# Loading q and k as bf16 through GpSimd's queue in place of fp32 loads and on-chip casts

## The chip, the cores and the metric

One Trainium2 chip, and of it one core with its engines TensorE (PE), VectorE (DVE), ScalarE (ACT), GpSimd (POOL) and SyncE (SP), and 16 DMA engines that all queues share. The metric is the device time of one execution in microseconds (us), lower is better. A ratio is the mean time of one kernel's fast runs over that of the other's fast runs of the same rounds, so it is not quite the ratio of the medians that stand beside it.

## The reference

Attention with a feature map, whose output is normalised, sent through two large matrices, and added back:

```python
def phi(x):                                  # per head, x is 576 x 64
    proj = einsum('bhsd,df->bhsf', x, w_phi)             # 64 -> 128
    proj = proj - max(abs(proj), axis=-1, keepdims=True)
    return concatenate([exp(proj), exp(-proj)], axis=-1)
q_p, k_p = phi(q), phi(k)                    # q, k, v: 8 x 8 x 576 x 64, fp32
kv, z = einsum('bhsf,bhsd->bhfd', k_p, v), sum(k_p, axis=2)
x = einsum('bhsf,bhfd->bhsd', q_p, kv) / (einsum('bhsf,bhf->bhs', q_p, z) + 1e-6)
x = x.transpose(0, 2, 1, 3).reshape(8, 576, 512)
xn = (x - mean) / sqrt(var + 1e-6) * g_ln
out = x + maximum(xn @ w_ch1, 0) @ w_ch2     # 512 -> 2048 -> 512
```

## The kernel before

The batch is taken in four pairs; a pair has eight units (a head of both batches, or two heads of one), so there are 32 units. A unit's rows are 8 main tiles (512 rows of each half) and a rest, the "tails". A planner in the kernel's own Python lays all instructions out: each operation states the engines that may do it, its estimated cost, what it reads and writes, and a rank; a table `OFF` moves single ranks. Each engine then runs its list strictly in order.

```python
def load_main(key, n, nu, rank, queue): ...   # fp32, SyncE's queue, for n >= 8 two units a load
def a_trans(u): ...        # units 0..7: TensorE turns the high halves of the fp32 tile

def a_trans_dma(u):        # units 8..31
    b16 = b16_bufs[n % 2]                       # two bf16 buffers
    def cast_main(engine, i):                   # i: q or k, 128 x 512
        cast(engine, b16[:, i * 512 : (i + 1) * 512]..., qk_bufs[u["g"] % NBUF][:, i : i + 1, u["hh"], :])
    def turn():
        nc.sync.dma_start_transpose(out=u["qkT"]..., in_=b16)
    add(("DVE", "ACT", "POOL"), (0.21, 0.19, 0.36), rank, cast_mixed, ...)        # tails
    for i in range(2):
        add(("DVE", "ACT", "POOL"), (0.61, 0.5, 0.98), rank, ... cast_main(engine, i), ...)
    dma("SP", rank, 1152, turn, ...)
...
def load_w2(n, V, gate): ...       # fp32 to bf16 during the load, GpSimd's queue, 512 KB
...
if n == EARLY:
    for j in range(NW):
        load_w2(j, -5 + j, [("came", "q", 5)])
    gate("w2", GATE)               # SyncE's loads for units 8.. wait until w2's first part is there
...
for key in "kqv":
    load_main(key, m, HG, rank, "SP")           # m = n + 4
```

On GpSimd's list stand also `vv`, the scaling of v (for both halves of each unit), and the puts of attention's result into `x`. Parts of one tile of x have to change partitions, by small copies `x<-xs` (32 KB each) on ACT's queue.

## Time and profile before

| | before |
|---|---|
| median of the first runs | 373.9 us |
| TensorE busy | 356.9 us, 96% |
| DVE, ACT, POOL busy | 292.2, 239.0, 175.5 us |
| main casts for units 8 to 31 | 48: 12 on DVE, 16 on ACT, 20 on POOL |
| POOL's issues | 8 weight loads, 780 ns each for those of w2 |
| TensorE's shown waits after the start | 5.9 us |

The page is read from the top: busy shares say who might be the bound, slices say when, and the views of waits and of the chain say what a wait of the bound engine ends on. In this kernel the two stretches before and after 140 us differ. Columns below: stretch, its length, busy us and count of PE, weight loads, DVE, ACT, POOL, then granted clock, share of the DMA engines, GB/s.

```profile
40.00:140.00 100.00, 95.55 (x1000) 63.40 (x1010) 88.09 (x204) 82.62 (x191) 69.55 (x146) 1.00 0.97 227
140.00:200.00 60.00, 57.24 (x611) 35.65 (x615) 53.67 (x115) 52.46 (x125) 40.74 (x80) 1.00 0.73 168
```

Up to 140 us the DMA column stands at 0.97; from there to 200 us at 0.73. It adds up the times of all packets as the profile records them. Packets can overlap, so it can pass 1 (it is 1.21 from 50 to 60 us); "full" below means a column near 1 or above. (Some matmuls are missing from this trace, so PE's 95.55 and 57.24 are a few us low.)

### The profile page before, as it was taken

The numbers are of one execution on the slowest core, as the hardware profiler recorded it, in microseconds if no ns is written. First come the engines' busy times: TensorE is split into PE (matmuls) and PEld (weight loads), VectorE is DVE, ScalarE is ACT, GpSimd is POOL, SyncE is SP. The second block draws the span as 40 slices with busy tenths as digits, with TensorE's granted clock in tenths as the row PEclk, the third lists the DMA queues.
The fourth block names the chain that finished last, engine by engine and source line by source line (L and its number), as shares of the span: only waits on it lengthen the run. The fifth ranks groups of instructions, "written<-read, shape, count | busy, mean of one in ns | idle before, by whom it ended". The sixth has DMA issues, their size and how long they took to land.

```text
span 373.1 us, 9310 instructions
## 1 busy us (share of the span) xinstructions
PE 356.9 (96%) x3510; PEld 229.7 (62%) x3548; DVE 292.2 (78%) x645; ACT 239.0 (64%) x569; POOL 175.5 (47%) x356
## 2 busy tenths in 40 slices
PE   8899998999999999989999999999999999999995
PEld 7789776666556556546656646666566555555543
DVE  6799988979599889989988898858687956454522
ACT  4798977568889999989878789835675540000000
POOL 2634848646668868746586754161728100000000
PEclk9999999999999999999999999999999999999999
DMA  6999399895999997596943439500100180110102
GB/s 184 274 200 338 63 205 286 248 265 123 257 260 221 249 256 207 158 208 153 223 80 90 130 98 176 120 8 24 56 2 31 36 204 0 42 45 30 56 28 87
DMA packets 92974, 53.38 MB, mean 143 GB/s; under 512 B 59392, under 2 KB 88448, under 8 KB 92928
## 3 DMA queue, kind: packets, MB, share of 16 engines
q1 hardware_dynamic: 87040, 48.19, 51.6%
q0 software_dynamic: 4224, 4.19, 6.8%
q10 hardware_dynamic: 1664, 0.39, 0.5%
q8 instruction: 28, 0.46, 0.5%
q14 instruction: 18, 0.15, 0.1%
HBM read 36.77 MB, written 9.44 MB: 124 GB/s over the span
## 4 chain that ended last, share of the span: by engine, by line
PE 70%; DMA 14%; DVE 6%; ACT 4%; SPq 2%; issue 2%; POOL 1%; DVEq 0%; ACTq 0%; POOLq 0%
PE hT_ps L1275 28%; PE ch_ps L1305 26%; DMA qkT<-b 4%; DMA qk<-in_k_dram 4%; PE n_bank L998 3%; PE num L1041 2%; PE pk L796 2%; PE pq L941 2%; SPq L509 2%; DMA xT<-xc 2%; DMA w<-in_moe_w_ch_dram 2%; DVE numc L1055 1%; DMA x<-xs 1%; DVE numc L1060 1%; PE pt L946 1%
## 5 line engine op out<-in xcount | busy, mean ns | idle before, releaser
L1275 PE MATMUL hT_ps<-xT,w 128*128 128x384 bf16 (+1 forms) x832 | 150.7, 313 | 2.9 <-ACT hT L1285 1.2
L1305 PE MATMUL ch_ps<-w,hT 128*128 128x512 bf16 (+1 forms) x554 | 138.8, 373 | 2.0 <-issue 0.3
L1275 PEld LDWEIGHTS <-w 128*128 128x128 bf16 x832 | 76.8, 98 | 49.7 <-issue 6.4
L1283 DVE TENSOR_SCALAR hT<-hT_ps 128x384 bf16<-128x384 f32 (+1 forms) x134 | 70.5, 529 | 42.5 <-PE hT_ps L1275 40.7
L1305 PEld LDWEIGHTS <-hT 128*128 128x128 bf16 x592 | 54.4, 98 | 45.7 <-issue 1.7
L1070 POOL TENSOR_TENSOR x<-numc,rden 128x192 bf16<-128x192 f32 (+4 forms) x112 | 49.5, 459 | 65.4 <-DVE rden L1064 60.3
L824 POOL TENSOR_TENSOR vv<-v,em 128x512 bf16<-128x512 f32 x59 | 61.6, 1047 | 31.0 <-ACT em L809 15.6
L812 ACT ACTIVATE eb<-pk 128x1024 bf16<-128x1024 f32 x64 | 64.8, 1041 | 7.2 <-DVE m L802 7.2
L1285 ACT ACTIVATE hT<-hT_ps 128x384 bf16<-128x384 f32 (+1 forms) x74 | 34.2, 467 | 53.6 <-PE hT_ps L1275 52.7
L965 ACT ACTIVATE ea<-pt 128x1024 bf16<-128x1024 f32 x56 | 57.3, 1035 | 12.2 <-PE pt L946 11.4
L802 DVE TENSOR_REDUCE m<-pk 128x8 f32<-128x1024 f32 x32 | 38.7, 1211 | 0.9 <-PE pk L796 0.9
L958 DVE TENSOR_REDUCE m<-pq 128x8 f32<-128x1024 f32 x28 | 34.1, 1217 | 2.9 <-PE pq L941 2.6
L1312 DVE SCALAR_TENSOR_TENSOR o<-ch_ps,rstd,x 128x512 f32<-128x512 f32 (+1 forms) x37 | 27.0, 731 | 10.2 <-PE ch_ps L1305 8.3
L1041 PEld LDWEIGHTS <-ea 128*128 128x128 bf16 x512 | 25.3, 97 | 7.3 <-issue 0.8
L1188 DVE BATCH_NORM_STATS2 st<-x 128x6 f32<-128x256 bf16 (+1 forms) x52 | 25.0, 512 | 2.4 <-DMA x<-xs 1.8
L998 PE MATMUL n_bank<-vv,eb 128*128 128x65 bf16 x512 | 26.8, 194 | 0.0
L712 POOL TENSOR_TENSOR b<-qk,one 128x512 bf16<-128x512 f32 x20 | 20.6, 1039 | 9.8 <-DMA qkT<-b 9.1
L837 POOL TENSOR_TENSOR vv<-vx,em 128x130 bf16<-128x130 f32 x60 | 24.2, 403 | 0.3 <-DMA vx<-in_v_dram 0.3
L998 PEld LDWEIGHTS <-eb 128*128 128x128 bf16 x512 | 22.3, 98 | 2.7
L1503 PE MATMUL n_bank<-wz 128*128 128x120 bf16 x295 | 22.8, 225 | 0.5 <-ACT KV L1007 0.5
L1212 ACT ACTIVATE xc<-x,mv 128x512 bf16<-128x512 bf16 x30 | 20.2, 719 | 2.4 <-DVE mv L1203 1.7
L1503 PEld LDWEIGHTS <-wz 128*128 128x128 bf16 x295 | 19.0, 103 | 1.1 <-issue 0.8
(92 smaller groups left out, 454.6 us busy)
## 6 DMA issues: line engine op xcount, KB each, us to landing
out_dram<-o SPq DMA_DIRECT2D x31, 256.0 KB, 2.8
qk<-in_k_dram SPq DMA_DIRECT2D x24, 256.0 KB, 4.4
v<-in_v_dram SPq DMA_DIRECT2D x24, 256.0 KB, 3.9
qk<-in_q_dram SPq DMA_DIRECT2D x24, 256.0 KB, 5.0
w<-in_moe_w_ch_dram POOLq DMA_DIRECT2D x8, 512.0 KB, 10.7
qk<-in_k_dram SPq DMA_DIRECT2D x4, 512.0 KB, 5.6
qk<-in_q_dram SPq DMA_DIRECT2D x4, 512.0 KB, 6.7
v<-in_v_dram SPq DMA_DIRECT2D x4, 512.0 KB, 5.0
```

Of the source, the lines that this page charges most:

```text
L802: nc.vector.reduce_max(out=u["m"][:, 1, 0:MX], in_=u["pk"], axis=AX.X, apply_absolute_value=True)
L812: nc.scalar.activation(u["EB"][:, t, 0:MX, :], u["pk"], AF.Exp, scale=(1.0, -1.0)[t])
L824: eng.tensor_tensor(out=u["vv"][:, t, 0:MX, 0:D], in0=vb[:, hh, :].rearrange("p (c d) -> p c d", d=D), in1=bcast(e[:, 0:MX], 2, D), op=ALU ...
L958: nc.vector.reduce_max(out=out, in_=ps, axis=AX.X, apply_absolute_value=True)
L965: nc.scalar.activation(u["EA"][:, t, :], u["pt", None], AF.Exp, scale=(1.0, -1.0)[t])
L998: nc.tensor.matmul(ps[:, t, c // 4, :], EB[:, t, c, :], vv[:, t, c, :], start=False, stop=(t == 0 and c == MX - 1), skip_group_check=True,)
L1070: nc.gpsimd.tensor_tensor(out=dst, in0=st["numc"][ps_, at, 0:D], in1=bcast(st["rden"][ps_, at], 2, D), op=ALU.mult,)
L1275: nc.tensor.matmul(st["ps"], w1_sb[:, kc, jj * P : (jj + 1) * P], xT_bufs[xj][:, kc : nt * KC : KC, :], start=(kc == 0), stop=(kc == KC - 1),)
L1283: nc.vector.tensor_relu(h_sb[:, 0 : nt * P], st["ps"])
L1285: nc.scalar.activation(h_sb[:, 0 : nt * P], st["ps"], AF.Relu)
L1305: nc.tensor.matmul(ch[t, c][:, cols], hT[jj][:, rt * P : (rt + 1) * P], w2_sb[:, jj, cols], start=(jj == 0), stop=(jj == JC - 1),)
L1503: nc.tensor.matmul(warm, wz, wz[:, 0:WN], start=False, stop=False, skip_group_check=True)
```

## The change

The intent: let the DMA engines convert q and k while they load, so that DVE, ACT and GpSimd are rid of 48 casts, and let nine bf16 places (three in each of the three fp32 tiles that the first pair no longer needs) replace two, so that a unit's data can be asked for long before its turn. The memory of the two bf16 buffers becomes a fourth v buffer. The core of the diff (line cuts by "..."; the whole table `OFF` is new as well, some 400 numbers, and lets the planner order the new work; two of the planner's rules for GpSimd's transfers changed with it):

```diff
-    NBUF = 3
+    NBUF, VB = 3, 4
...
-    b16_bufs = [consts.tile([P, ST], BF16, name=f"b16_{i}") for i in range(2)]
...
+    def place(n):
+        i = (n - QK_DMA) % (3 * NBUF)                      # QK_DMA is 8
+        return i, (i // 3 + 1) % NBUF
+    def b16_of(n): ...                                     # that place in qk_bufs, as bf16
+    def load_cast(key, n):
+        src = bass.AP(tensor=t.tensor, ..., ap=[[4 * D, P], [...], [1, 4 * D]])     # 256 rows of 1 KB
+        first = n < QK_DMA + 5
+        dma("POOL", -3.5 + 0.1 * (n - QK_DMA) if first else rk("load." + key, n), 256,
+            lambda: nc.gpsimd.dma_start(out=dst, in_=src),
+            r=[("came", "q", 5) if first else ("turned", n - 5)] + freed(n), w=[("b16", i, slot)],
+            us=0.6, ns=0.05)
...
-        for i in range(2):
-            add(("DVE", "ACT", "POOL"), (0.61, 0.5, 0.98), rank, lambda engine, i=i: cast_main(engine, i), ...)
...
-                load_w2(j, -5 + j, [("came", "q", 5)])
+                load_w2(j, (-5.0, -4.0, -3.25, -3.15)[j], [("came", "q", 5)])
...
-            for key in "kqv":
-                load_main(key, m, HG, rank, "SP")
+            load_main("v", m, HG, rank, "SP")
+        if H <= m < NU:
+            for key in "kq":
+                load_cast(key, m)
```

`us=0.6, ns=0.05`: the planner takes an issue to cost GpSimd 0.6 us and a packet 50 ns.

## The prediction

> **What bounds the kernel now.** I read the page's busy times and slices first, then the engines over three stretches, then the costliest groups, the waits, and the chain of waits.
>
> The page (busy time, share, count; then the span in 40 slices, in tenths):
>
> ```profile
> PE 356.9 (96%) x3510; PEld 229.7 (62%) x3548; DVE 292.2 (78%) x645; ACT 239.0 (64%) x569; POOL 175.5 (47%) x356
> ...
> PE   8899998999999999989999999999999999999995
> ...
> DMA  6999399895999997596943439500100180110102
> ```
>
> Busy time by stretch (PE, weight loads, DVE, ACT, POOL, clock, DMA share, GB/s):
>
> ```profile
> 40.00:240.00 200.00, 192.48 (x2002) 123.41 (x2022) 178.20 (x395) 170.04 (x392) 131.62 (x262) 1.00 0.81 188
> 240.00:300.00 60.00, 59.52 (x546) 35.32 (x553) 47.10 (x101) 35.35 (x85) 25.97 (x49) 1.00 0.12 35
> ```
>
> TensorE is the bound from 40 us to the end, at full clock; from 40 to 240 us the engines that feed it are not far behind (DVE 89%, ACT 85%, POOL 66%). The first 36 us are set by loads and the chain of the first heads: 295 warm-up matmuls (L1503, 22.8 us) fill them. The reader should then ask how much TensorE really lacks. The waits in which TensorE stood still:
>
> ```profile
> PE n_bank L993 <- DVE numc L1060: 1.9, 2, 1.7
> PE qkT_ps L645 <- DMA qk<-in_k_dram: 1.5, 2, 1.3
> PE hT_ps L1275 <- ACT hT L1285: 1.2, 1, 1.2
> ...
> PE hT_ps L1275 <- DVE hT L1283: 0.9, 1, 0.9
> PE n_bank L1041 <- ACT ex L771: 0.7, 1, 0.7
> ```
>
> After the start, shown waits come to only 5.9 us (1.9 + 1.2 + 0.9 + 0.7 + 0.4 + 0.3 + 0.3 + 0.2). The timeline of TensorE gives a second bound. Its first expert matmul starts at 36.7 us, its last ends at 365.2: 328.5 us. Back to back in the trace, four hT matmuls of 384 columns take 0.65 us, sixteen of 256 take 1.75, three of 512 take 0.65. So the expert part needs 640 x 0.1625 + 192 x 0.109 + 576 x 0.216 = 249 us, and attention of 28 head pairs about 2.43 us each (timeline near 140 us: q 0.55, kv 0.64, k 0.44, mixed 0.17, num 0.63) = 68 us. 328.5 - 317 leaves **11.5 us: the most that any relief of the other engines can give**, and part of it is small gaps at changes of matmul kind that no relief takes away.
>
> What the change touches:
>
> ```profile
> L712 POOL TENSOR_TENSOR b<-qk,one 128x512 bf16<-128x512 f32 x20 | 20.6, 1039 | 9.8 <-DMA qkT<-b 9.1 <-DMA qk<-in_k_dram 0.7
> L710 ACT CAST b<-qk 128x512 bf16<-128x512 f32 x16 | 10.0, 631 | 5.4 <-DMA qkT<-b 5.3
> L706 DVE TENSOR_REDUCE b<-qk 128x512 bf16<-128x512 f32 x12 | 8.1, 674 | 3.5 <-DMA qkT<-b 2.4 <-DMA qk<-in_k_dram 1.1
> L612 POOL DMA_DIRECT2D w<-in_moe_w_ch_dram x4 | 3.0, 780 | 0.0
> ```
>
> 48 main casts, with idle time before them that ends with a transpose: two bf16 buffers make each cast wait for the transpose of two head pairs earlier. The chain of waits passes there too:
>
> ```profile
> 41.72 5.92 DMA w<-in_moe_w_ch_dram
> 47.65 0.68 SPq L521
> 48.39 9.43 DMA qk<-in_k_dram
> ...
> 86.90 4.05 DMA qkT<-b
> ...
> 96.27 5.58 DMA qkT<-b
> ```
>
> The second pair's q and k start only when the first part of w2 has landed (SyncE's gate at 47.65).
>
> **What the Trainium skill says.** "DMA: Bandwidth & Descriptors", section "SWDGE vs HWDGE vs iDMA": a cast during a transfer goes only through GpSimd's queue, where software writes the descriptors. The trace agrees as far as it goes: the only casting loads, the weights, are issued by POOL and take 780 ns of it for 512 descriptors. The same page, "Issuing engines are not separate DMA queues": all queues share the same 16 DMA engines, so moving loads from SyncE saves issue time, not bandwidth. "SBUF — State Buffer", section "Who interferes with whom": a DVE instruction in a two-port mode (copy, cast, tensor_scalar from SBUF) shuts GpSimd out, descriptors included; tensor_reduce does not. Here only the few xc<-x instructions of the first pair (L1207, 340 ns) look like that, so I expect little of it. "Perfetto Trace Analysis", section "Identifying the Most-Contended Engine": matmul busy time is a poor measure of headroom. The trace agrees: 96% busy hides about half of the 11.5 us.
>
> **The change part by part.**
> Removed: 12 casts from DVE (8.1 us), 16 from ACT (10.0), 20 from POOL (20.6). Between 40 and 240 us DVE falls from 178 to about 170, ACT from 170 to 160. The 24 small casts of tails stay.
> Added: 48 loads issued by POOL, 256 descriptors each. The weight load costs 780 ns for 512, so one costs between 390 and 780 ns; I estimate 0.6 us, 29 us in all (19 to 37). POOL nets +8 us (-2 to +17), from 66% to about 70% of that stretch: not a bound.
> DMA: the same fp32 bytes are read. A weight packet costs 96 ns (6.8% of 16 x 373.1 us over 4224 packets) for 2 KB read, so a 1 KB one about 48 ns, an estimate: 12,288 of them fill 37 us of all 16 engines, about as before. Nothing saved.
> Moved: q and k have nine bf16 places in place of two, and up to five head pairs are requested ahead; the first ten loads are no longer behind SyncE's gate and can start near 43 us. Cast and transpose leave the chain. The fourth v buffer loosens v's loads. POOL issues six of the q/k loads between the second and third w2 parts, and the fourth w2 part after two head pairs' vv work.
> Start: the order of instructions has 11 more warm-up matmuls before the first expert matmul: 11 x 0.0525 = **+0.6 us**.
> Gain: faster evictions and an earlier q/k recover about half of the shown 5.9 us and a little of the small gaps: **-3.5 us**. It can't be more than perhaps 8.
> A new wait: in the built order each load of POOL's queue, from the ninth on, waits for the semaphore of the load eight before it. The third w2 part thus waits inside POOL for the first w2 part to land (5.9 us after its issue before), with vv of the next head pair behind it. And w2's last two parts land behind q/k loads in the same queue, when before the fourth landed 15.8 us after its issue, just as its first matmuls came near 62 us. I put **+0.6 us** on this: most of it is caught by other expert work.
> Sum: +0.6 - 3.5 + 0.6 = -2.3; 373.9 - 2.3 = **371.6 us**.
>
> **Rivals.**
> 1. POOL's queue becomes the wait. For it: the eight-deep semaphores, loads and vv in one in-order queue, w2's tight arrival. Against it: POOL idles 5.1 us at 51 to 56 us before, and 60 us in total before its x work. If w2's late parts hold TensorE, 3 to 6 us at 55 to 70 us are lost: 375 to 378.
> 2. The relief is fuller: DVE at 89% is a second bound, and all its gaps close. For it: every long wait of TensorE ends with DVE or ACT. Then -7 to -8 and no new wait: 366. Against it: the largest one (1.7 us at 167) came while DVE worked on other things in a poor order, and re-tuned ranks can do as badly.
> 3. The casts were hidden: TensorE had other work, and nothing changes: 373 to 374. For it: the load of 9.43 us and the cast's waits lie on the chain, yet TensorE is idle only 1.7 us between 40 and 60.
>
> **Range and chances.** The cap of 11.5 us less the unavoidable small gaps puts faster by over 2% (below 366.4) at 1 in 10; a loss of over 2% (above 381.3) needs a stall of 10 us with nothing recovered: 1 in 20. Eight in ten: 366.5 to 377.
>
> **What would show it.** Right: no b<-qk groups; DVE near 170 and ACT near 160 us between 40 and 240; 48 POOL issues of about 0.6 us; waits on qkT<-b before casts gone; TensorE's shown waits after the start near 3 us; first expert matmul near 37.3 us. Wrong: an issue costing 1 us or more; a wait of TensorE on w2 near 60 us; vv late behind issues; a start more than 1.5 us off, as all order ranks were tuned anew, which the parts above don't cover.

## The result and the profile after

The changed kernel took **385.75 us** (384.36 to 387.33, four runs) against 373.48 us: ratio 1.0321, 95% interval 1.0261 to 1.0382. It is slower by 3.2%, outside the range of the prediction. Executions over 1.5% slower than the fastest of the same kernel are left out of the means.

The page of the changed kernel, the lines that answer to those of before:

```profile
PE 361.3 (94%) x3559; PEld 231.0 (60%) x3559; DVE 287.3 (75%) x630; ACT 233.0 (61%) x549; POOL 193.8 (50%) x391
...
PE   8899988868989899999999999999999999999995
...
DMA  6998399990699999998977508315100252110102
```

and the same stretches:

```profile
40.00:240.00 200.00, 185.80 (x1942) 118.71 (x1940) 164.79 (x364) 156.58 (x359) 147.12 (x294) 0.99 0.86 151
240.00:300.00 60.00, 60.00 (x598) 36.21 (x596) 49.42 (x102) 36.30 (x82) 24.72 (x45) 1.00 0.21 44
```

```profile
40.00:140.00 100.00, 85.86 (x933) 58.19 (x931) 79.26 (x187) 74.92 (x172) 75.90 (x158) 0.98 0.91 156
140.00:200.00 60.00, 59.95 (x618) 36.42 (x615) 52.32 (x113) 51.80 (x119) 50.00 (x98) 1.00 0.96 169
```

DVE and ACT did fall, to 165 and 157 us between 40 and 240. (Part of that is only that the stretch held less work: over the whole span DVE fell by 4.9 and ACT by 6.0 us, where 8.1 and 10.0 us of casts had been taken away.) But TensorE is idle for 14 us of the hundred from 40 to 140, while from 140 to 200 it is busier than before (59.95 us). So the change did two opposite things in two stretches, and only the first decides. Its waits:

```profile
PE pk L828 <- DVE m L990: 4.2, 1, 4.2
PE hT_ps L1307 <- ACT hT L1317: 2.1, 3, 1.0
...
PE n_bank L1025 <- POOL vv L869: 1.8, 2, 1.5
...
PE n_bank L786 <- DMA qkT<-qk: 1.5, 1, 1.5
```

The largest ends on DVE. DVE was not the limit there, though: it runs in order, and stood before an instruction that waited for a transfer. The page has it, after and before (the last number is the idle time that ended with this transfer):

```profile
L1220 DVE BATCH_NORM_STATS2 st<-x 128x6 f32<-128x256 bf16 (+1 forms) x52 | 25.4, 515 | 7.4 <-DMA x<-xs 5.5
```

```profile
L1188 DVE BATCH_NORM_STATS2 st<-x 128x6 f32<-128x256 bf16 (+1 forms) x52 | 25.0, 512 | 2.4 <-DMA x<-xs 1.8
```

The chain of waits of the changed kernel shows what lies behind it (start, duration, what; cut):

```profile
43.00 5.99 DMA w<-in_moe_w_ch_dram
49.00 0.69 SPq L528
...
51.87 9.27 DMA qx<-in_q_dram
...
75.19 4.34 DMA v<-in_v_dram
79.61 6.41 DMA x<-xs
86.03 1.02 DVE st L1220 x2
87.16 1.10 DVE m L990
88.30 1.01 PE pk L828 x4
```

Read it upwards from TensorE's 88.30: it waited for a maximum on DVE, DVE for `x<-xs`, a copy of 32 KB that took 6.41 us from issue to landing (before, the four copies of this kind took 3.1 to 4.9 us). Above it a v load of 4.34 us, and above that the tails of q, 64 KB, 9.27 us on their way. These are small transfers that crawl. What fills the DMA engines meanwhile is seen when the queues are listed for 50 to 70 us: software queue q0 (GpSimd's) and hardware queue q1; packets, MB, share of the 16 engines. Before:

```profile
q1 hardware_dynamic: 5811, 3.66, 65.7%
q0 software_dynamic: 1057, 1.04, 30.9%
```

After:

```profile
q0 software_dynamic: 4031, 2.63, 86.9%
q1 hardware_dynamic: 3284, 1.59, 44.5%
```

In packet time GpSimd's queue takes 87% of the 16 engines there, and both queues together 131%, against 97% before. In halves: 121% and 78% before, 133% and 135% after; the crowd is longer, rather than new. That packets wait for each other shows in the smallest: q1's packets of 256 bytes took 20 ns on average in this stretch before, and 38 ns after (from the packet records of the traces, which no view lists by size). (MB counts what is written, half of what a casting load reads.) The clock makes TensorE pay a second time. The stretch of the wait and the one after it:

```profile
84.00:88.00 4.00, 0.15 (x1) 0.00 (x0) 1.97 (x4) 0.71 (x1) 0.00 (x0) 1.00 0.63 97
88.00:90.00 2.00, 1.70 (x8) 1.05 (x8) 2.00 (x8) 1.22 (x6) 0.00 (x0) 0.51 0.00 0
```

TensorE idles 4 us, and then runs at 0.51 of its clock (0.64 in the 2 us that follow): some 1.7 us more (2 x 0.49 + 2 x 0.36). The Trainium skill, "TensorE: Matmul & The Clock Gate", section "What's actually happening", says that after one idle window of about 3.4 us the clock is halved; this trace agrees.

What a casting load costs its issuer, from the view of its line (min, median, max in ns; then issue to landing in us):

```profile
L598 POOL DMA_DIRECT2D qk<-in_k_dram x24: 706/716/762, 44.5 to 209.0; - x24
L598 POOL DMA_DIRECT2D qk<-in_q_dram x24: 716/762/771, 45.2 to 208.3; - x24
...
DMA to landing us min/median/max: 3.0/6.0/12.7
```

About 0.74 us each, 35 us in all, for 256 rows; a w2 load of 512 rows takes 0.78. And the cost to the DMA engines: q0 held 20.5% of 16 x 384.0 us = 1260 us for 17,280 packets; less the weights (4224 x 96 ns = 405 us, the packet time of before) that is 855 us for 13,056 packets, **65 ns each**. The loads that they replaced were q1's: its time fell from 51.6% of 16 x 373.1 us (3080 us) to 41.0% of 16 x 384.0 us (2519 us), and its packets by 12,928: 43 ns each, if q1's other packets cost the same in both kernels. They don't, so this figure is too low. The packet records, sorted by size, give the price itself: **52 ns** on average for an fp32 packet of 1 KB before, **68 ns** for one of the 12,288 casting packets (medians 46 and 60; 65 ns above because it includes 768 packets of 4 bytes). So the same reads cost about a third more, 12,288 x 16 = 197 us or 12 us of all 16 engines. In all, the packet time of both queues grew by 855 - 561 = 294 us, 18 us of all 16 engines; most of the rest is q1's other packets, which got slower.

**A ruler for the rest.** From the timeline of TensorE I took, at each moment, the time gone less what the matmuls issued so far need back to back (warm-up ones count as nothing). This "lost time" does not depend on the order of the work, and says where a kernel fell behind. One profile of each kernel; single profiles differ by about 1 us for no reason, and a recount from the packed traces, with slightly other times for a matmul, moves the two "lost" columns by up to 1.1 us.

| kernel | at 40 us | at 140 us | at 350 us | lost 40 to 140 | lost 140 to 350 |
|---|---|---|---|---|---|
| before | 22.9 | 31.6 | 38.6 | 8.7 | 7.0 |
| after | 24.4 | 44.9 | 48.5 | 20.5 | 3.6 |

So the start costs 1.5 us (part of it chance, see below), the stretch from 40 to 140 costs 11.8 us, and the rest gives 3.4 us back (11.6 and 2.3 us in the recount).

### The profile page after: what moved, and what is told of

It reads as the page before. It is cut to its first block, busy times and chain, and to the rows that moved or that the text cites. A ratio compares the mean times of both kernels' runs of the same rounds, so it can differ in the third digit from the quotient of the medians.

```text
span 384.0 us, 9310 instructions
## 1 busy us (share of the span) xinstructions
PE 361.3 (94%) x3559; PEld 231.0 (60%) x3559; DVE 287.3 (75%) x630; ACT 233.0 (61%) x549; POOL 193.8 (50%) x391
## 3 DMA queue, kind: packets, MB, share of 16 engines
q0 software_dynamic: 17280, 10.49, 20.5%
## 4 chain that ended last, share of the span: by engine, by line
PE 70%; DMA 14%; POOL 5%; SPq 4%; DVE 3%; ACT 2%; issue 1%; DVEq 0%; ACTq 0%; POOLq 0%
PE ch_ps L1337 27%; PE hT_ps L1307 25%; DMA qkT<-qk 4%; PE n_bank L1030 3%; SPq L516 3%; DMA qx<-in_q_dram 3%; PE pk L828 3%; PE num L1073 2%; PE n_bank L1537 2%; POOL vv L856 2%; POOL x L1102 2%; DMA x<-xs 2%; PE pq L973 2%; DMA qk<-in_k_dram 2%; DMA w<-in_moe_w_ch_dram 2%
## 5 line engine op out<-in xcount | busy, mean ns | idle before, releaser
L1337 PE MATMUL ch_ps<-w,hT 128*128 128x512 bf16 (+1 forms) x592 | 149.9, 375 | 0.6 <-DVE hT L1315 0.6
L1315 DVE TENSOR_SCALAR hT<-hT_ps 128x384 bf16<-128x384 f32 (+1 forms) x137 | 72.0, 528 | 45.6 <-PE hT_ps L1307 44.1
L856 POOL TENSOR_TENSOR vv<-v,em 128x512 bf16<-128x512 f32 x60 | 62.7, 1045 | 42.5 <-issue 18.6
L1317 ACT ACTIVATE hT<-hT_ps 128x384 bf16<-128x384 f32 (+1 forms) x71 | 32.5, 457 | 65.7 <-PE hT_ps L1307 65.2
L1244 ACT ACTIVATE xc<-x,mv 128x512 bf16<-128x512 bf16 x32 | 21.8, 734 | 6.7 <-DVE o L1344 5.1
L1030 PEld LDWEIGHTS <-eb 128*128 128x128 bf16 x512 | 22.3, 98 | 5.5 <-issue 2.2
L869 POOL TENSOR_TENSOR vv<-vx,em 128x130 bf16<-128x130 f32 x63 | 25.2, 400 | 0.0
L1537 PE MATMUL n_bank<-wz 128*128 128x120 bf16 x306 | 23.7, 228 | 0.6 <-ACT KV L1039 0.5
L828 PE MATMUL pk<-wbk,qkT 128*128 128x256 bf16 x128 | 19.8, 279 | 4.2 <-DVE m L990 4.2
L1537 PEld LDWEIGHTS <-wz 128*128 128x128 bf16 x306 | 20.1, 105 | 0.7 <-issue 0.5
```

The source lines that it names most:

```text
L856: eng.tensor_tensor(out=u["vv"][:, t, 0:MX, 0:D], in0=vb[:, hh, :].rearrange("p (c d) -> p c d", d=D), in1=bcast(e[:, 0:MX], 2, D), op=ALU ...
L1030: nc.tensor.matmul(ps[:, t, c // 4, :], EB[:, t, c, :], vv[:, t, c, :], start=False, stop=(t == 0 and c == MX - 1), skip_group_check=True,)
L1315: nc.vector.tensor_relu(h_sb[:, 0 : nt * P], st["ps"])
L1337: nc.tensor.matmul(ch[t, c][:, cols], hT[jj][:, rt * P : (rt + 1) * P], w2_sb[:, jj, cols], start=(jj == 0), stop=(jj == JC - 1),)
L1537: nc.tensor.matmul(warm, wz, wz[:, 0:WN], start=False, stop=False, skip_group_check=True)
```

## The experiments

Theories: **1**, GpSimd's issue time: ten issues of 0.74 us stand among w2, v scaling and x puts in one in-order list. **2**, the casting transfers: they take 65 ns a packet in place of some 50, in a burst, where the DMA engines are full. **3**, the new order (`OFF`) costs by itself. **4**, added later: the planner laid the order out for loads cheaper than they are. Thirteen kernels ran.

### Swapping the order tables

`r1` is the kernel before with the new table, `r2` the changed kernel with the old one.

```diff
 r1, r2
-OFF = { ... its own ... }
+OFF = { ... the other kernel's ... }        # r2 keeps "load.k", "load.q"
```

> The kernel before, with only the table of offsets of the changed kernel (the order in which the engines take their work), fp32 loads and casts kept. The changed kernel is 12.3 us slower than before (385.8 against 373.5). If the new order itself is what costs (theory 3), this kernel should rise to 380 us or more. If GpSimd's issue time (theory 1) or the transfer time of the casting loads (theory 2) is the cause, the order is worth little by itself: 372 to 377 us.

> The changed kernel with the table of offsets of the kernel before (only the entries for the new loads kept). Theory 3 (the new order costs): back to 373 to 377 us. Theories 1 and 2 (issue time on GpSimd's queue, transfer time of casting loads): 383 to 390 us, as both causes are still in it.

Measured: r1 406.61 us (ratio to before 1.0839), r2 391.94 us (1.0461). Both are slower than either kernel. By the letter of its expectation r1 (380 us or more) speaks for theory 3, and r2 lies above both of its bands. But both tables cost time in the kernel that they were not searched for, so I take r1 to say nothing of what the order costs in the changed kernel. r2 does say that going back to the old order is no cure: the new order is worth some 5 us to the changed kernel (1.0461 against 1.0321). Theory 3 in its plain form falls.

### GpSimd's issues alone

`y1` adds to the kernel before ten casting loads of 64 bytes a row, at about the places of the first ten.

```diff
+    def tiny_loads(c0, c1):
+        for c in range(c0, c1):
+            src = bass.AP(tensor=k.tensor, ..., ap=[[4 * D, P], [S * D, 2], [1, 16]])
+            nc.gpsimd.dma_start(out=tiny[c], in_=src)
 ...
+            if n == 1: tiny_loads(0, 6)            # behind the second w2 part
+            if n == 5 and t == 0: tiny_loads(6, 10)    # behind vv of unit 5
```

> The kernel before in its own order, with ten more casting loads on GpSimd's queue at the places where the changed kernel has its first ten: six behind the second w2 part, four behind the v scaling of unit 5. Each has 256 descriptors of 64 bytes into a tile that nobody reads, so GpSimd pays the whole issue (10 x 0.74 = 7.4 us) and the DMA engines next to nothing. Theory 1 (issue time ahead of the v scaling and x puts): TensorE loses most of these 7.4 us between 45 and 90 us, 378 to 382 us. Theory 2 (transfer time): at most 1 us, 373 to 375 us.

Measured: 379.06 us, ratio 1.0093 (1.0039 to 1.0147), about 3.5 us. The profile names one wait of TensorE:

```profile
53.09 0.22 PE L1006 MATMUL n_bank<-vv,eb 128*128 128x130 bf16 x1 [3.41 <-POOL vv L848]
```

and on GpSimd, just before that v scaling:

```profile
50.70 0.74 POOL L621 DMA_DIRECT2D w<-in_moe_w_ch_dram  x1 [2.75 <-DMA w<-in_moe_w_ch_dram]
```

GpSimd stood 2.75 us before the fourth w2 issue, because a ninth load of its queue waits for the load eight before it, here an earlier w2 part; v scaling stood behind. So theory 1 is real in the old order: 3.5 us, a good part of it that wait and not the issues themselves. (The tiny loads were not free as transfers: GpSimd's queue has 2,720 packets and some 76 us of packet time more, 4.8 us of all 16 engines. How much of the 3.5 us is theirs is not shown.)

### The transfers made cheap, the issues kept

`n1` and `n2` are the changed kernel in its own order, whose first ten loads (units 8 to 12) copy bf16 values out of w1's tile in SBUF. Their outputs are wrong, which doesn't matter for the times. `n1` has one contiguous kilobyte a partition, `n2` two rows of 512 bytes.

```diff
 n1
-            lambda: nc.gpsimd.dma_start(out=dst, in_=src),
+            lambda: nc.gpsimd.dma_start(out=dst, in_=w1_sb[:, 0, 0:512]... if first else src),
 n2
+            lambda: nc.gpsimd.dma_start(out=dst, in_=w1_sb[:, 0:2, 0:256] if first else src),
```

> The changed kernel in its own order, where the first ten casting loads copy bf16 values out of the w1 tile in SBUF instead of casting q and k from HBM (512 bytes a descriptor, same 256 descriptors, same issues on GpSimd; the result is wrong on purpose). Theory 1: issue time is as before, so 384 to 387 us. Theory 2: the DMA engines no longer saturate from 50 to 70 us, tails and v land on time, 374 to 379 us. In between, the share of each is the part of 12.3 us that goes.

> The run with cheap transfers gained 8 us, but its issues also took 0.56 instead of 0.74 us (one contiguous kilobyte a partition), and its start fell 1.6 us earlier, though nothing differs up to there. Here the ten loads copy two separate rows of 512 bytes a partition from the w1 tile, so each has 256 descriptors as the casting load has and GpSimd should pay 0.7 us or more. If the transfers were the cause (theory 2), the time stays at 376 to 379 us. If the shorter issues were (theory 1), it goes back to 382 to 386 us.

Measured: n1 378.02 us (1.0100), n2 378.31 us (1.0100, 1.0063 to 1.0137), against 1.0321 for the changed kernel: **8 us less**. In n1 the issues had shrunk to 0.56 us, which left a doubt; in n2 they take 0.7 to 0.74 us as in the changed kernel, and the time is the same. GpSimd's queue has 106 us less of the 16 engines (19.2% of 16 x 375.3 us against 1260), 6.6 us of all of them. The wait of before is nearly gone in n2's profile:

```profile
PE pk L828 <- DVE m L990: 0.9, 1, 0.9
```

since `x<-xs` was issued 4.1 us earlier (75.47) and landed in 4.4 us in place of 6.4, and the clock stays at 1.00. Lost time from 40 to 140 falls from 20.5 to 12.3 us; in the recount, 4.9 us of that difference lie between 84 and 90 us, in the one stall and the slow clock behind it. So the transfers of the first ten loads carry two thirds of the loss.

What n1 and n2 take away is more than the conversion. In the trace a cheap load is 32 packets of 4 KB where a casting load is 256, and it reads nothing from HBM. So they show what ten transfers cost at this place. They don't show whether ten plain fp32 loads at the same place would cost less (the price of a packet), or ten casting loads held behind SyncE's gate (the place). No run tried either.

A word on the start: n1 and n2 don't differ from the changed kernel up to 43 us, yet their first expert matmul falls at 36.9 and 37.3 us, the changed kernel's at 38.4 and that of before at 36.7. So some 1 us of the 1.5 us at the start is chance.

### Neither issue nor casting transfer; all sixteen cheap; only four cheap

`n3` issues the same ten cheap copies from SyncE. `m2` makes all sixteen loads of the second pair cheap. `m1` makes cheap only the four (units 13 and 15) that are issued right beside `x<-xs`.

```diff
 n3
+            lambda: nc.sync.dma_start(out=dst, in_=w1_sb[:, 0:2, 0:256]) if first else nc.gpsimd.dma_start(out=dst, in_=src),
 m2
+            lambda: nc.gpsimd.dma_start(out=dst, in_=w1_sb[:, 0:2, 0:256] if n < 16 else src),
 m1
+            lambda: nc.gpsimd.dma_start(out=dst, in_=w1_sb[:, 0:2, 0:256] if n in (13, 15) else src),
```

> The changed kernel, where the first ten loads take neither GpSimd's time nor a casting transfer: the same SBUF copies of 512 byte rows from w1, issued by SyncE's queue (the result is wrong on purpose). If issue time (some 3.5 us) and transfers (some 8 us) together are the whole loss, this falls from 385.8 to the time of before or a little under it, 371 to 375 us. If another part of the change costs too (the fourth v buffer, the order, the waits of the later loads), it stays at 377 us or more.

> As the run with ten cheap transfers (378.3 us), but all sixteen loads of the second pair are cheap SBUF copies, issued by GpSimd as before (the result is wrong on purpose). If transfers of the casting loads carry the whole loss: 371 to 375 us. If GpSimd's issue time carries a real part of it in this order: 376 us or more.

> The changed kernel, where only the four loads that GpSimd issues from 77.6 to 80.5 us (units 13 and 15), right beside the small copy x<-xs (issued 79.6, landed 6.4 us later), copy rows of 512 bytes from the w1 tile; the first ten are real casting loads again (the result is wrong on purpose). If TensorE's 4.15 us wait for m and the fall of the clock after it come from these four sharing the queues with x<-xs: 379 to 382 us, and x<-xs lands within 4 us. If the loss is all in the first burst: 384 to 386 us.

Measured: n3 379.39 us (1.0128, 1.0048 to 1.0207), m2 378.57 us (1.0094), m1 384.09 us (1.0206, 1.0113 to 1.0300; 380.9 to 386.2). Three readings follow.

- n3 is not below n2. In the changed kernel's own order, taking the ten issues off GpSimd, onto SyncE's list, gained nothing measurable: the 1.5 us wait of TensorE for v scaling on GpSimd is gone from the profile, but TensorE now waits 2.9 us on the `x<-xs` path (5.8 us on its way). The 3.5 us of y1 can't simply be added to the 8 us.
- m2 is not below n2 either: once the first burst is cheap, the later loads of the pair cost nothing measurable. Its expectation had put 376 us or more down to GpSimd's issue time; n3, which has none for the first ten, is no faster, and speaks against that.
- m1 is unclear. Its profile shows the same stall (5.4 us of DVE for `x<-xs`, 3.6 of TensorE), but it is the profile of the slowest of four executions, 386.2 us; two others took 380.9 and 382.1 us, which is what was expected if these four loads were the cause. So I had probably read the trace wrongly, and the four loads beside `x<-xs` are not what delays it, but that is not shown. A reading that fits the profiles: the first burst delays the three transposes (SyncE is done issuing them at 73 us; at 69 in n2), tails and v follow late, and the small copy then meets those.

Some 3.5 to 4.8 us (1.0094 to 1.0128) remain that no cheapening took away.

### The loads held back

`p2` keeps the result right and moves issues: units 11 and 12 behind v scaling of unit 8, where 14 already stood, units 13 and 15 behind that of unit 9.

```diff
+    HOLD, kept = {11: 8, 12: 8, 13: 9, 15: 9}, {}       # 14 already stood behind unit 8
 ...
-            lambda: nc.gpsimd.dma_start(out=dst, in_=src),
+            lambda: held(n, lambda: nc.gpsimd.dma_start(out=dst, in_=src)),
```

(The text on record tells units 14 and 15 the wrong way round: in the kernel that ran, 14 stands behind unit 8 and 15 behind unit 9.)

> The changed kernel with a right result, where GpSimd issues the loads of units 11 and 12 (in the burst at 53 to 59 us) and of 13 and 15 (at 77 to 80 us) later: 11, 12 and 15 behind its v scaling of unit 8, at some 88 us, 13 and 14 behind that of unit 9; nothing else is moved. If the crowding of these transfers with tails, v and x<-xs is what costs: 376 to 381 us. If bytes and issues cost the same wherever they stand: 384 us or more. A new wait of the transposes of units 11 to 15 for their loads would show as TensorE waiting for qkT after 97 us.

Measured: 385.69 us (1.0274, 1.0206 to 1.0343): next to no gain. The stall at 84 us is gone, at 90 us TensorE has lost 32.0 us in place of 39.9, and then this:

```profile
105.55 0.39 PE L794 MATMUL n_bank<-wbk,qkT 128*128 128x256 bf16 x1 [6.96 <-DMA qkT<-qk]
```

The transpose of unit 11 was issued at 96.8 us and took 8.7 us, beside ten casting loads from 87.5 to 97.4. The time is that of the rival that I had named for the run ("bytes and issues cost the same wherever they stand"), and the wait is the new one that the expectation had named. It can be read as the crowd, only moved, that delays another small transfer. But the loads held back are also the data that unit 11's transpose needs, so p2 does not separate a crowd from data that come late.

### The plan made with the real costs

`t2` tells the planner 0.74 us and 66 ns, at most eight of GpSimd's loads under way, and has its `OFF` searched anew by the planner's own estimate.

```diff
-            us=0.6, ns=0.05)
+            us=0.74, ns=0.066)
```

> The changed kernel, whose planner is told what the trace shows: 0.74 us on GpSimd for one casting issue (it had 0.6), 66 ns for one of its packets (50), 0.78 us for a weight issue, and at most eight of GpSimd's loads under way; the offsets were searched anew under these costs. Theory 4 (the loss is one of planning: the order was laid out for loads cheaper than they are): most of the 12.3 us comes back, 375 to 380 us. Theories 1 and 2 in their hard form (the issues and bytes cost this wherever they stand): 383 us or more. Below 372 us the change would be a gain after all.

Measured: 382.71 us over runs from 377.4 to 386.4, the two of four that count as fast at ratio 1.0128 (1.0047 to 1.0209). Unclear: some of the loss may be of planning, but no plan found here brings the changed kernel to the time of before.

### What the casts were worth

`c1` is the kernel before, whose main casts from unit 10 on convert 8 columns, with all loads, waits and order kept. Its output is wrong, which doesn't matter for the time.

```diff
+        few = 512 if n < H + 2 else 8
-                engine, b16[:, i * 512 : (i + 1) * 512]..., qk_bufs[...][:, i : i + 1, u["hh"], :],
+                engine, b16[:, i * 512 : i * 512 + few]..., qk_bufs[...][:, i : i + 1, u["hh"], 0:few],
```

> The kernel before, with loads, order and waits kept, whose casts of main tiles from the third on convert 8 columns instead of 512 (the result is wrong on purpose; the stale rest is what units 8 and 9 left). It measures by itself what the change was to gain. If the relief is as the prediction has it: 3.5 us, so about 370 us. If the casts were hidden beside TensorE (the prediction's third rival): 372.5 to 374 us. The changed kernel made up about 2 us between 140 and 350 us, which speaks for 371 to 372.

Measured: 372.72 us, ratio 0.9962 (0.9909 to 1.0016): 1.4 us at best estimate, and no gain isn't excluded; the time lies in the band of the prediction's third rival, that the casts were hidden. By lost time, 2.6 us less at 350 us, 1.8 of it after 140 us. From 40 to 140 us, where I had looked for the gain, the casts were all but hidden (0.5 us).

### Half of the change

`h4` and `h5` load the second pair as the kernel before does, and only pairs three and four through GpSimd's queue, with three v buffers; results are right. `h4` has a newly searched order; `h5` keeps the order of before up to 86 us.

```diff
+    FIRST = 16
 ...
+        if n < FIRST: ... cast_main as before ...
 ...
-            load_main("v", m, HG, rank, "SP")
-        if H <= m < NU:
+            for key in "kqv" if m < FIRST else "v":
+                load_main(key, m, HG, rank, "SP")
+        if FIRST <= m < NU:
```

> A version that might beat both: the second pair is loaded as fp32 on SyncE's queue and cast on chip as in the kernel before, and only the third and fourth pair are loaded as bf16 by GpSimd's queue; three v buffers; the planner has the measured costs and offsets searched anew. The changed kernel gained about 2 us after 140 us, when the queues have room. If that gain stands without the loss: 371 to 373 us. If the casts of the later pairs were hidden too, or the new order is worse than the old one: 374 to 379 us.

> As the version with half of the change (374.1 us, no different from before), but with the order of the kernel before kept up to 86 us by the planner, so that nothing of the start and of the second pair differs; only the third and fourth pair are loaded as bf16 by GpSimd's queue. If the loss lies wholly in the loads of the second pair and the gain of dropping casts is real (1.4 us in the run without main casts, some 3 us of TensorE's lost time after 140 us in the half change): 370 to 372.5 us. If casting loads cost something in the quiet stretch too, or the gain is only of the order: 373 to 376 us.

Measured: h4 374.09 us (0.9970, 0.9910 to 1.0029), h5 **373.21 us against 374.83** (0.9943, 0.9897 to 0.9990; five rounds). h5 is ahead of the kernel before, by 0.6% (one of its six runs, 377.4 us, counts as slow and is left out of the ratio). By the letter of its expectation 373.2 us fell in the band "casting loads cost something in the quiet stretch too, or the gain is only of the order". The second half of that stays possible: its order after 86 us was searched anew, and the kernel before was not searched again beside it. Its stretches:

```profile
40.00:140.00 100.00, 96.55 (x1039) 65.11 (x1048) 90.59 (x206) 84.05 (x200) 79.49 (x173) 1.00 0.95 200
140.00:200.00 60.00, 58.55 (x605) 36.31 (x612) 52.87 (x117) 48.04 (x108) 45.05 (x84) 1.00 0.84 142
```

Nothing is lost up to 140 us. Each casting packet costs it 66 ns too (16.5% of 16 x 370.1 us, less 405, over 8704), so the 65 ns are not the crowd's doing. And 15 of its 32 casting loads are issued between 91 and 140 us, where the DMA column stands at 0.95, without a loss; in the changed kernel TensorE is busy for 59.95 of 60 us from 140 to 200 us at a column of 0.96. So a full column alone does not make a casting load costly. What only the changed kernel has is ten of them within 15 us, beside w2, the tails, v and the transposes. Which part of that it takes was not tried. The lost time of all that matter:

| kernel | at 40 us | at 140 us | at 350 us | lost 40 to 140 | lost 140 to 350 |
|---|---|---|---|---|---|
| y1, ten tiny issues in before | 22.3 | 35.0 | 41.6 | 12.7 | 6.6 |
| n2, ten cheap transfers | 23.4 | 35.7 | 40.7 | 12.3 | 5.0 |
| n3, the same from SyncE | 23.7 | 37.5 | 42.1 | 13.8 | 4.6 |
| p2, loads held back | 23.0 | 43.1 | 47.8 | 20.1 | 4.7 |
| c1, before without main casts | 22.6 | 30.8 | 36.0 | 8.2 | 5.2 |
| h5, half of the change | 23.3 | 30.7 | 36.1 | 7.4 | 5.4 |

## Why the prediction was wrong

By its own steps:

- **The bound and the cap.** The bound was right: TensorE, with little to gain. The cap of 11.5 us rests on a misread end: by the timeline the last expert matmuls end at 368.9 us, not 365.2, which makes it some 15 us. Nothing hung on it, as no run came near either. DVE and ACT fell to 165 and 157 us between 40 and 240 (it said 170 and 160), in part because that stretch held less work.
- **"+0.6 us" at the start.** Right within chance: +0.2 to +1.7 us for the first expert matmul in kernels alike up to there.
- **The issue, "I estimate 0.6 us, 29 us in all".** Too low: 0.74 us, 35 us. The step split the time of 512 rows by rows; it is nearly all fixed (256 rows 0.74, 512 rows 0.78). The Trainium skill, "DMA: Bandwidth & Descriptors", section "Anatomy of one DMA — SWDGE (gpsimd) path", says that many descriptors can be made before their cost shows; the traces agree, and I had not drawn the consequence.
- **"a 1 KB one about 48 ns ... about as before. Nothing saved."** This is the step that failed. The 48 ns were scaled from a packet of another size, and were not held against what the replaced packets cost. Measured: 68 ns against 52, so 52 us of all 16 engines for the 48 loads where the step had 37, in place of 40. The step had asked whether bytes are saved, not whether a transfer that converts is slower, nor that the ten loads let loose "near 43 us" fall where the engines are already full; the early start was counted as a gain alone. All this entered the sum with 0; n2 shows 8 us for the transfers of these ten loads. How much of that is the price and how much the place stays open.
- **"-3.5 us" of gain.** Too large, and not clearly there at all: c1 has 1.4 us with no gain inside its interval, and by lost time after 140 us it is 1.6 (h5) to 3.4 us (the changed kernel). Nearly nothing came before that. So rival 2 (a fuller relief, 7 to 8 us) is out, and rival 3 (the casts were hidden) is nearer the truth than the sum.
- **"+0.6 us" for the new wait.** Right mechanism, wrong size: the queue of eight with v scaling behind it costs up to 3.5 us in the old order (y1). In the changed kernel's own order it is the 1.5 us wait for `vv`, and taking the issues away did not shorten the whole (n3).
- **Rival 1**, "POOL's queue becomes the wait", came nearest, but put it on w2's late parts at 55 to 70 us and at 3 to 6 us. The largest wait was at 84 us, for the tails, v and `x<-xs`, in the DMA engines behind the queue, and the loss twice as much. The prediction gave a stall of 10 us 1 in 20.

What stays open: of the 11.8 us lost between 40 and 140 us, n2 accounts for 8.2. The other 3.6 us are split between issue time, the eight-deep queue and the order in ways that the runs don't separate, as each removal let another wait grow. The fourth v buffer was not tried alone: it does not fit beside the kernel before.

## What to carry to other kernels

A conversion moved into the DMA engines is not free there: price a transfer by a packet of its own kind and compare it with the packet that it replaces, in the stretch where it will run, not over the whole span. Ask too what else is under way when the new loads are let loose: ten of them at once, among small transfers that others wait for, cost 8 us here, while fifteen spread over 50 us cost nothing that the ruler shows, though the DMA column was near 1 or above it in both places. When a burst is moved and the time stays, look for the new small transfer that now stands in it.

## What the Trainium skill lacked or had wrong

- "DMA: Bandwidth & Descriptors" says that a cast during a transfer goes through GpSimd, not what it costs: 68 ns a packet here against 52 for the plain fp32 load of the same reads, 12 us more of all 16 engines for 48 loads of 128 KB written.
- The same page puts descriptor making at "small, variable"; it lacks the time that GpSimd is taken by one issue: 0.74 us for 256 rows, 0.78 for 512 (0.56 where each partition's kilobyte was contiguous in SBUF).
- The same page gives times of single transfers, but under load only the latency of one HBM access: 32 KB took 3.1 to 4.9 us from issue to landing before and 2.6 to 7.3 us after, 64 KB of tails 9.3 us, a transpose 8.7 us.
- I found no page that tells of the wait of GpSimd's ninth load for the load eight before it (a matter of how the program was built): 2.75 us in y1.
